# A one-core transformer block: a fixed issue order in place of a list scheduler, with four changes to the work itself

## The chip, the cores and the metric

The kernel runs on one core of a Trainium2 chip. The metric is the device time of one execution in microseconds (us). A run of this program on one core has no second die to compare with; runs are called fast or slow by the spread of the same kernel's times (over 1.5% above its fastest is slow), and only fast runs are compared. The profile's span (first to last instruction) is about 1.7 us shorter than the reported time: 214.4 us against 216.15 us in the profiled run of the kernel before.

Engines in the profile: PE is TensorE's matmuls, PEld its weight loads, DVE is VectorE, ACT is ScalarE, POOL is GpSimd. A name with q (POOLq) is an engine's sequencer.

## The reference

One transformer block in bf16, on x of 2048 rows by 512, modulated by a vector c:

```python
mod = (silu(c) @ w_mod)                       # six rows of 512: sa, ca, ga, sb, cb, gb
h = layernorm(x) * (1 + ca) + sa              # first norm
x = x + ga * A(h)                             # A: 32 heads of 16; each row looks at 8 rows,
                                              #    0, 2, ..., 14 rows back; softmax; @ wo
h = layernorm(x) * (1 + cb) + sb              # second norm
x = x + gb * B(h)                             # B: third norm, then an MLP that mixes ROWS:
                                              #    gelu(h^T @ w1 + b1) @ w2 + b2
                                              #    w1 [2048, 1792], w2 [1792, 2048]
```

The MLP mixes rows, so its first product sums over all 16 tiles of 128 rows, and its gelu cannot start before the last tile has passed the third norm. The 1792 hidden columns are 14 units of 128.

## The kernel before: what the change and the argument touch

The kernel describes its work as operations on engines and lets a list scheduler with hand-tuned ranks (`RANK`, `BIAS`) put them in order and, where it may, choose the engine. Chunks of 2, 4, 4, 4 and 2 tiles pass through norm, QKV, attention and output projection; the sums of MLP1 run in between.

ScalarE computes each 1/sqrt(variance) as Exp(-0.5 Ln(v)), and each softmax's reciprocal as Exp(-Ln(s)). One explicit table load, with nothing to wait for, stands first on ScalarE; the set that it names holds both Ln and Exp:

```python
add("act", 1.3, lambda: nc.scalar.add_instruction(
    mybir.InstLoadActFuncSet(name=..., act_func_set_id=6, ins=[], outs=[])), name="act_table")

def ln_rstd(l, g0, n, name, ...):             # l: which of the three norms
    def fa():
        nc.scalar.activation(lv[:, sl, 0], var, ACT.Ln, bias=epscol[:, 0:1])
        nc.scalar.activation(rs[:, sl, 0], lv[:, sl, 0], ACT.Exp, scale=-0.5)
    add("act", 0.5, fa, ...)
    if vreads is None and "A" not in NE[l][g0:g0 + n]:
        return                                # normalise as (x - mean) * rs
    ...                                       # else nb = -mean * rs, normalise as x * rs + nb

# softmax: (cut)
nc.scalar.activation(ls, ps(s_s)[:, 0:SB], ACT.Ln)
nc.scalar.activation(rb, ls, ACT.Exp, scale=-1.0)
```

`NE` holds a letter for each norm and tile: A for ScalarE, D for VectorE, P for GpSimd. MLP1 is summed in sweeps over tiles; between sweeps a unit's partial sum is parked in SBUF, and taken up again by a matmul with the identity (`inj`) or by an addition on VectorE (`padd`):

```python
BOUNDS=(6, 10)                                # all 14 units are parked after tiles 6 and 10
bounds = [0] + list(BOUNDS) + [NST]
for li, (s_lo, s_hi) in enumerate(zip(bounds[:-1], bounds[1:])):
    ...                                       # load w1's rows, then for each of the 14 units:
    for s in range(s0, s1):
        nc.tensor.matmul(ps(s_), lhsT=w1p[:, s - s_lo, fl * P:(fl + 1) * P], rhs=h3[:, s, :], ...)
...
order = G.schedule()                          # the list scheduler
for o in order:
    o.fn()
```

## Time and profile before

| kernel before | |
|---|---|
| time, median of 3 runs | 216.18 us (216.0 to 216.32) |
| span in the profile | 214.4 us |
| third chunk's row maximum done | 61.68 us |
| last tile normed, last PE stretch begins | 148.99 us |
| work of PE behind it, and tail | 61.5 us and 3.9 us |
| table loads on ScalarE | 2 |

From the page of the kernel before: busy time of each engine, and the chain of work that ended last, by engine.

```profile
PE 201.8 (94%) x1453; PEld 99.9 (47%) x1475; DVE 168.1 (78%) x256; ACT 123.9 (58%) x270; POOL 24.2 (11%) x43
...
PE 73%; DVE 15%; DMA 4%; issue 3%; ACT 1%; POOLq 1%; SPq 1%; DVEq 0%
```

The shares are averages over stages with different limits. The end of the chain of waits of the kernel before shows the last stage (start, duration, engine, tile, instructions):

```profile
143.43 3.28 issue
146.71 2.24 POOLq L1082
148.99 4.26 PE psS L238 x19
...
197.55 12.95 PE psS L238 x73
```

The last norm, on GpSimd, is done at 148.95 us (146.71 + 2.24); PE starts at 148.99 and works without a hole until 210.5. So the span is the time T of the last normed tile, plus the PE work behind it, plus a tail: 149.0 + 61.5 + 3.9. Before T, two engines share the load. The table of windows of the kernel before (window; its length and then the busy us of PE, PEld, DVE, ACT, POOL with their instructions; granted clock; DMA share; GB/s):

```profile
15.00:30.00 15.00, 14.95 (x111) 9.56 (x111) 14.08 (x29) 11.59 (x25) 4.22 (x3) 0.90 1.02 277
30.00:45.00 15.00, 13.99 (x135) 6.55 (x136) 13.12 (x14) 11.44 (x23) 6.12 (x4) 1.00 0.41 98
45.00:60.00 15.00, 14.89 (x139) 6.70 (x138) 14.58 (x9) 10.97 (x22) 0.00 (x0) 1.00 0.99 150
```

PE and VectorE are nearly full; ScalarE has 3 to 4 us free in each 15. The row maximum of each chunk's attention is a good clock hand of this stretch, as it stands between VectorE's products and ScalarE's Exp. In the timeline of VectorE before (start, duration, ...):

```profile
26.39 0.67 DVE L238 TENSOR_REDUCE m<-psL 128x64 bf16<-128x512 f32 x1
47.56 1.22 DVE L238 TENSOR_REDUCE m<-psL 128x128 bf16<-128x1024 f32 x1 [0.36 <-PE psL L238]
60.46 1.22 DVE L238 TENSOR_REDUCE m<-psL 128x128 bf16<-128x1024 f32 x1
```

And the first instructions of ScalarE before; in brackets the idle time ahead of an instruction, and what ended it:

```profile
1.38 1.28 ACT L238 ACT_TABLE_LOAD   x1 [1.38 <-PEq L1071]
4.70 0.29 ACT L238 ACTIVATE lv<-mv,epscol 128x2 f32<-128x2 f32 x1 [2.03 <-POOL stack L238]
5.02 0.20 ACT L238 ACTIVATE rs<-lv 128x2 f32<-128x2 f32 x1
```

`lv` is the Ln of a norm, `rs` its Exp. The table is loaded while ScalarE has nothing else to do, and Exp follows Ln at once.

### The profile page before, as it was taken

How to read it: one execution, taken by the hardware profiler on the slowest of the kernel's cores; microseconds unless marked ns; L12 is line 12 of the kernel's file. 1: busy time of each engine (PE TensorE's matmuls, PEld its weight loads, DVE VectorE, ACT ScalarE, POOL GpSimd, SP SyncE). 2: the span in 40 equal slices, each digit the busy share in tenths (PEclk: the TensorE clock that was granted, in tenths of full speed). 3: DMA queues.
4: the chain of work that ended last, by engine and by line, in shares of the span. 5: the costliest groups of instructions: out<-in, count | busy, mean ns of one | idle time of the engine just before them, and what ended most of it. 6: DMA issues, size and time to landing. Idle time of an engine off the chain costs nothing.

```text
span 214.4 us, 3880 instructions
## 1 busy us (share of the span) xinstructions
PE 201.8 (94%) x1453; PEld 99.9 (47%) x1475; DVE 168.1 (78%) x256; ACT 123.9 (58%) x270; POOL 24.2 (11%) x43
## 2 busy tenths in 40 slices
PE   7599999899999999999999999988999999999992
PEld 7479345335444447443443344333444444444451
DVE  3699999799999999999999789997854445544553
ACT  3548778658789989988857668886852000000000
POOL 6030709100000000000000034034000000000000
PEclk9958999999999999999999999999999999999998
DMA  5999974359999999999999886449879110111011
GB/s 170 355 351 333 206 210 101 90 124 161 148 130 134 134 137 311 134 131 135 223 272 207 220 222 174 127 97 321 203 181 249 49 45 28 54 49 49 24 49 50
DMA packets 54182, 34.24 MB, mean 160 GB/s; under 512 B 18452, under 2 KB 54164, under 8 KB 54164
## 3 DMA queue, kind: packets, MB, share of 16 engines
q1 hardware_dynamic: 54156, 34.00, 74.6%
q8 instruction: 11, 0.18, 0.4%
q14 instruction: 7, 0.06, 0.1%
q10 hardware_dynamic: 8, 0.00, 0.0%
HBM read 22.03 MB, written 2.10 MB: 113 GB/s over the span
## 4 chain that ended last, share of the span: by engine, by line
PE 73%; DVE 15%; DMA 4%; issue 3%; ACT 1%; POOLq 1%; SPq 1%; DVEq 0%
PE psS L238 69%; DVE st L238 4%; DVE h L238 4%; PE psL L238 4%; DVE big L238 4%; DMA xx<-in_A_x_dram 3%; DMA hT<-h 2%; DVE mv L238 1%; POOLq L1082 1%; DVE xx L238 1%; SPq L238 1%; DVE w_qkv L238 0%; ACT lv L238 0%; ACT o_sb L238 0%; ACT k_f L238 0%
## 5 line engine op out<-in xcount | busy, mean ns | idle before, releaser
L238 PE MATMUL psS<-h,wst 128*128 128x512 bf16 x216 | 50.9, 379 | 1.7 <-POOL h L238 1.2
L238 PE MATMUL psS<-hT,w_qkv 128*128 128x512 bf16 (+1 forms) x234 | 47.1, 346 | 1.2 <-DMA hT<-h 0.9
L238 PEld LDWEIGHTS <-wst 128*128 128x128 bf16 x324 | 30.3, 99 | 35.4 <-issue 4.1
L238 PEld LDWEIGHTS <-w_qkv 128*128 128x128 bf16 x282 | 29.8, 114 | 23.7 <-issue 5.8
L238 DVE TENSOR_TENSOR big<-a2sb,vD 128x4096 bf16<-128x4096 bf16 (+1 forms) x20 | 37.0, 1863 | 2.0 <-DMA vD<-v_f 1.5
L238 DVE TENSOR_TENSOR big<-q_sb,k_f 128x4096 bf16<-128x4096 bf16 (+1 forms) x20 | 36.8, 1859 | 0.2 <-ACT k_f L238 0.2
L238 DVE SCALAR_TENSOR_TENSOR h<-psS,bcol,gb_bc 128x512 f32<-128x512 f32 (+1 forms) x17 | 12.2, 719 | 24.6 <-PE psS L238 24.5
L238 ACT ACTIVATE gT<-psS 128x512 bf16<-128x512 f32 x28 | 15.9, 591 | 5.2 <-PE psS L238 5.2
L238 PE MATMUL psS<-gT,big 128*128 128x512 bf16 x83 | 18.2, 379 | 0.1
L238 DVE BATCH_NORM_STATS2 st<-xx 128x6 f32<-128x512 bf16 x21 | 14.2, 675 | 4.2 <-DMA xx<-in_A_x_dram 4.1
L238 PE MATMUL psS<-woq,o_sb 128*128 128x512 bf16 x61 | 16.2, 380 | 0.2
L238 PE MATMUL psS<-gT,wst 128*128 128x512 bf16 (+1 forms) x83 | 15.3, 343 | 0.1
L238 PEld LDWEIGHTS <-big 128*128 128x128 bf16 x116 | 9.2, 98 | 12.3 <-DMA big<-in_w_mod_dram 2.4
L238 ACT ACTIVATE h<-xx,nb,rs 128x512 bf16<-128x512 bf16 x17 | 13.3, 809 | 1.8 <-DVE nb L238 1.7
L238 PEld LDWEIGHTS <-ident 128*128 128x128 bf16 (+1 forms) x146 | 11.1, 110 | 6.8 <-issue 1.7
L238 POOL TENSOR_SCALAR h<-xx,mv,rs 128x512 bf16<-128x512 bf16 x2 | 4.3, 2132 | 87.5 <-DVE xx L238 87.0
L238 ACT ACTIVATE q_sb<-psS,qvb 128x512 bf16<-128x512 f32 (+1 forms) x20 | 11.7, 605 | 4.0 <-PE psS L238 3.9
L238 DVE TENSOR_TENSOR psS<-psS,gT 128x512 f32<-128x512 f32 x14 | 9.2, 695 | 4.6 <-PE psS L238 4.6
L238 ACT ACTIVATE v_f<-psS,qvb 128x512 bf16<-128x512 f32 (+1 forms) x20 | 11.5, 601 | 1.1 <-PE psS L238 0.7
L238 POOL TENSOR_SCALAR h<-xx,rs,nb 128x512 bf16<-128x512 bf16 x7 | 10.3, 1485 | 15.3 <-DMA woq<-in_A_wo_dram 8.6
L238 ACT ACTIVATE k_f<-psS 128x512 bf16<-128x512 f32 x16 | 9.5, 597 | 4.0 <-PE psS L238 3.7
L238 ACT ACTIVATE lv<-mv,epscol 128x1 f32<-128x1 f32 (+2 forms) x25 | 7.3, 292 | 7.9 <-DVE mv L238 5.7
(96 smaller groups left out, 234.9 us busy)
## 6 DMA issues: line engine op xcount, KB each, us to landing
vD<-v_f SPq DMA_DIRECT2D x48, 130.0 KB, 7.4
wst<-in_B_w_dram SPq DMA_DIRECT2D x6, 768.0 KB, 5.6
wst<-in_B_w_dram SPq DMA_DIRECT2D x4, 896.0 KB, 5.8
big<-in_B_w_dram SPq DMA_DIRECT2D x3, 896.0 KB, 6.3
vD<-v_f SPq DMA_DIRECT2D x32, 66.0 KB, 3.6
out_dram<-h SPq DMA_DIRECT2D x15, 128.0 KB, 1.7
xx<-in_A_x_dram SPq DMA_DIRECT2D x3, 512.0 KB, 9.7
gT<-in_w_mod_dram SPq DMA_DIRECT2D x3, 512.0 KB, 9.4
```

Source lines behind the costliest of these rows:

```text
L238: r = fn(*a, **k)
L1082: with _tile.TileContext(nc) as tc:
```

## The change

The list scheduler, its ranks and its timing model are replaced by a table of some 800 names, `ORDER`; the order was evidently found by a search outside the kernel. Four changes of the work come with it:

- Units 0 to 6 of MLP1 are parked after tiles 6 and 10 as before, units 7 to 13 only once, after tile 9: seven `inj` matmuls and seven parkings less.
- The first group of MLP2 is issued in three runs, so that it can start before the last gelus are done; the last output tile is cut into pieces of 256, 128 and 128 columns.
- The four modulation rows, needed on all 128 partitions, were made by 16 broadcast matmuls of 512 columns. Now 64 one-column matmuls give the columns, and a round trip through DRAM spreads them as rows.
- The sums of the second norm are taken on ScalarE for all tiles but 14 and 15 (before: all but 10, 11, 12, 14, 15), and the letters of `NE` change: 14 norms on GpSimd. With them goes a rule: only a group of tiles that is all on VectorE still normalises as (x - mean) * rs; before, a group without ScalarE did, so that GpSimd had norms of both forms.

```diff
     def schedule(self):
-        ops = self.ops
-        ...                                  # list scheduling by ready time and rank (cut)
+        by_name = {o.name: o for o in self.ops}
+        for pos, token in enumerate(ORDER.split()):
+            name, *rest = token.split(":")   # name, and a or d for the engine
+            ...
+            order.append(o)
+ORDER = """
+ident ld_c ld_x_1 ld_x1 ld_x0 consts ld_wmod1 ld_wmod0 ld_wqkv2 cps ld_wqkv0 silu_exp silu_dve ln1s5 ld_wqkv1
+... (cut)
+ld_b1 n1_15 mrowt1 qkv3_10 pv1_1 vd1_31 mrows1:a act_table red2_3 vd1_01 qkv3_20 st_row1 ev3_02:a xt15 qkv3_00
+... (cut)
+"""
-    BOUNDS=(6, 10),
+    MIX=((0, 7, (6, 10)), (7, 14, (9,))),
-    NE=('AADADAPPPAAPPPAP', 'AAAAADDADAPDPAAA', 'DADDDDDDAAAAPDPD'),
-    X1D=(10, 11, 15),
-    LN2D=(10, 11, 12, 14, 15),
+    NE=('DAAADDAAAPAAPAAA', 'APPPAAADAAAPPPPP', 'PPAPAADDAPDADDDD'),
+    X1D=(14, 15),
+    LN2D=(14, 15),
-        if vreads is None and "A" not in NE[l][g0:g0 + n]:
+        if vreads is None and NE[l][g0:g0 + n] == "D" * n:
             return
-                    nc.tensor.matmul(ps(s_), lhsT=sc_rep[:, kt, :], rhs=src[:, kt, :], ...)   # 16 x 512 columns
+                            nc.tensor.matmul(ps(s_)[:, r * KT + dt_:r * KT + dt_ + 1],
+                                             lhsT=w_[:, dt_ * P:(dt_ + 1) * P], rhs=sc[:, kt:kt + 1], ...)
+            dma(scratch rows <- mrows), dma(rows_bc <- scratch, read 128 times)               # shortened
+            runs = [(0, 9), (9, 12), (12, NFT)] if st == 0 else [(0, NFT)]
```

`act_table` stands in `ORDER` after `mrows1:a`. The list scheduler had it first.

## The prediction

> **What bounds the kernel before.** The page gives PE 94%, DVE 78%, ACT 58% of a 214.4 us span. By stage (the table of 6 us windows) there are two limits. From 18 to 149 us DVE is full (5.6 to 6.0 of most windows) and PE nearly so; ACT has slack (46 us busy in the first 66). The chain of waits runs on DVE from 124 to 143, then waits for GpSimd's norm of a last tile until 149.0. After that PE alone counts: 61.5 us of back-to-back 512-column matmuls (219 ns apart), then a 3.9 us tail.
>
> So span = T (last normed tile) + PE work behind it + tail = 149 + 61.5 + 3.9.
>
> **What the change does, costed.**
> - PE: 16 broadcast-row matmuls and 7 injections go (23 x 0.219 = 5.0 us), 64 one-column ones come (2.5 us): -2.5 us, nearly all before T, where PE will have room.
> - DVE before T: three fewer statistics of the second norm (0.8 each), fewer norms; four hT copies and small sums more: about -3 us. ACT takes three sums of squares, GpSimd 14 norms instead of 9 (0.8 us alone, 2.1 when DVE is busy).
> - MLP1 by unit: half the units have a last sweep of 7 tiles, issued as one piece. In PE's order 91 MLP1 and 224 MLP2 matmuls stand behind the last normed tile: 315 x 0.219 = 69 us instead of 61.5, +7.4 us at unchanged T.
> - Split of the first MLP2 group, and 128-column last pieces: about -0.4 us of tail.
> - Table loads: the explicit load of the table with both Ln and Exp stood first on ACT; now it stands behind some 85 ACT instructions, and the built program has 17 table loads instead of 2: until then one before every Ln and every Exp. The Trainium skill ("ScalarE: Activation LUTs", "What ACT_TABLE_LOAD costs") gives 1283 ns plus a drain of 1380; the trace agrees with the first (1.28 us) and shows no such drain. 15 x 1.28 = 19 us more on ACT, all before about 62 us. ACT's slack there was about 20 us, so ACT becomes as full as DVE; each early norm and softmax gets 2.6 us of latency. I estimate the first QKV matmuls 3 us later, and the third chunk's max at 64.5 us (61.6 before). PE may also stay at half clock past 18 us, as its start is emptier.
>
> **Sum.** From the third max DVE needs 77 us (80 before) to the last normed tile, plus 4 to 8 idle (7.6 before): T = 146 to 150. Then 69 + 3.5: span 218 to 222. Without the table loads the same order would give about 212. The order was evidently searched and may pack better than my idle guess; I shade down: 219 us, 80% in 210 to 227. Faster 18%, same 36%, slower 46%.
>
> **What would show it.** ACT_TABLE_LOAD x17; ACT over 90% busy from 15 to 62 us; PE holes early, half clock longer; last normed tile near 147; then an unbroken PE stretch of 69 us; 14 norms on GpSimd; no broadcast-row matmuls.
>
> **What would make it wrong.** Table loads hidden because ACT's queue ran ahead of need (then 212 or less); DVE idle near zero after 60 us; or the last norms, now serial on GpSimd at 2.1 us, or the transfers of v's shifts pushing T beyond 150.

## The result

| | before | after |
|---|---|---|
| time, median | 216.2 us (216.0 to 216.32, 4 runs) | 225.57 us (225.32 to 226.09, 4 runs) |
| ratio of fast runs | 1 | 1.0438 (95%: 1.0415 to 1.046) |
| span in the profile | 214.4 us | 224.1 us |
| third maximum done | 61.68 us | 70.62 us |
| last PE stretch begins (T) | 148.99 us | 152.19 us |
| PE work behind it, and tail | 61.5, 3.9 us | 68.2, 3.7 us |

Ratios here and below are the mean time of one kernel's fast runs over that of the other's fast runs of the same rounds, so not quite the ratio of the medians.

The kernel is 4.4% slower. The same parts of the page, after, and with them the line of one group (count; busy us; mean ns; idle before and what ended it):

```profile
PE 200.9 (90%) x1504; PEld 103.1 (46%) x1528; DVE 166.2 (74%) x265; ACT 135.1 (60%) x281; POOL 19.0 (8%) x45
...
PE 47%; DVE 26%; ACT 15%; issue 7%; DMA 3%; DVEq 0%; ACTq 0%; SPq 0%
...
L131 ACT ACT_TABLE_LOAD x17 | 21.8, 1283 | 6.0 <-DVE mv L131 4.3 <-PEq L989 1.4
```

PE has 0.9 us less to do and the span is 9.7 us longer: this is not a matter of more work on PE. ScalarE's share of the chain went from 1% to 15%. There are 17 table loads. The first instructions of ScalarE after show where:

```profile
1.39 1.28 ACT L131 ACT_TABLE_LOAD   x1 [1.39 <-PEq L989]
...
7.19 1.28 ACT L131 ACT_TABLE_LOAD   x1 [4.33 <-DVE mv L131]
8.48 0.30 ACT L131 ACTIVATE lv<-mv,epscol 128x2 f32<-128x2 f32 x1
8.80 1.28 ACT L131 ACT_TABLE_LOAD   x1
10.09 0.20 ACT L131 ACTIVATE rs<-lv 128x2 f32<-128x2 f32 x1
```

Without the explicit load at the front, the build put a load before every Ln and every Exp until the explicit one comes at 67.16 us: 14 loads in seven pairs. Each holds ScalarE for 1.28 us. The bracket of the second line is worth a look: the load put in before the Ln stands behind the wait for the statistics (`mv`). So it does not run in the 4.33 us in which ScalarE is idle, but after them. (Ahead of the other pairs ScalarE was hardly idle, so only this one shows it.)

The windows after, the maxima after (timeline of VectorE), and a line of the waits over the whole span (engine, what it waited for; us in total, times, longest):

```profile
15.00:30.00 15.00, 12.99 (x82) 9.75 (x85) 10.91 (x36) 12.63 (x23) 2.41 (x5) 1.00 0.56 153
30.00:45.00 15.00, 12.27 (x81) 5.32 (x82) 12.24 (x11) 14.21 (x22) 3.79 (x1) 1.00 0.95 150
45.00:60.00 15.00, 11.99 (x166) 6.27 (x169) 14.15 (x13) 12.94 (x22) 0.00 (x0) 0.94 0.67 116
```

```profile
37.94 0.68 DVE L131 TENSOR_REDUCE m<-psL 128x64 bf16<-128x512 f32 x1
49.88 1.22 DVE L131 TENSOR_REDUCE m<-psL 128x128 bf16<-128x1024 f32 x1
69.40 1.22 DVE L131 TENSOR_REDUCE m<-psL 128x128 bf16<-128x1024 f32 x1
```

```profile
DVE nb L131 <- ACT rs L131: 9.9, 5, 3.6
```

From 15 to 60 us ScalarE is busy 39.8 of 45 us, VectorE 37.3 (41.8 before) and PE 37.3 (43.8 before). No engine is full: they wait for one another. VectorE alone waits 9.9 us for `rs`, nearly all of it for an Exp behind two table loads; in the kernel before this wait is 0.7 us in all. The end of the chain after:

```profile
152.19 7.93 PE psS L131 x36
...
214.13 6.29 PE psS L131 x56
```

From the third maximum to T the kernel after takes 81.6 us (152.19 - 70.62), the kernel before 87.3 (148.99 - 61.68). So 8.9 of the 9.7 us are lost before the third maximum. After it 5.7 us come back before T, and 6.7 us more of PE work stand behind T.

### The profile page after: what moved, and what is told of

Read it like the earlier page. It is cut to its first block, busy times and chain, and to the rows that moved or that the text cites. A ratio compares the mean times of both kernels' runs of the same rounds, so it can differ in the third digit from the quotient of the medians.

```text
span 224.1 us, 3994 instructions
## 1 busy us (share of the span) xinstructions
PE 200.9 (90%) x1504; PEld 103.1 (46%) x1528; DVE 166.2 (74%) x265; ACT 135.1 (60%) x281; POOL 19.0 (8%) x45
## 4 chain that ended last, share of the span: by engine, by line
PE 47%; DVE 26%; ACT 15%; issue 7%; DMA 3%; DVEq 0%; ACTq 0%; SPq 0%
PE psS L131 45%; DVE big L131 11%; DVE st L131 6%; DVE h L131 5%; ACT L131 5%; ACT h L131 3%; DVE mv L131 2%; PE psL L131 2%; DMA xx<-in_A_x_dram 2%; DMA vD<-v_f 1%; ACT q_sb L131 1%; ACT junk L131 1%; DVE m L131 1%; ACT xx L131 1%; ACT lv L131 1%
## 5 line engine op out<-in xcount | busy, mean ns | idle before, releaser
L131 PE MATMUL psS<-hT,w_qkv 128*128 128x512 bf16 (+1 forms) x230 | 47.6, 348 | 3.9 <-ACT k_f L131 2.6
L131 PEld LDWEIGHTS <-wst 128*128 128x128 bf16 x354 | 31.1, 99 | 35.7 <-issue 4.3
L131 DVE SCALAR_TENSOR_TENSOR h<-psS,bcol,rows_bc 128x512 f32<-128x512 f32 (+2 forms) x18 | 12.4, 690 | 23.4 <-PE psS L131 14.7
L131 ACT ACT_TABLE_LOAD x17 | 21.8, 1283 | 6.0 <-DVE mv L131 4.3
L131 PE MATMUL psS<-gT,wst 128*128 128x512 bf16 (+2 forms) x97 | 15.3, 317 | 0.1
L131 ACT ACTIVATE gT<-psS,bcol 128x512 bf16<-128x512 f32 x14 | 8.9, 686 | 10.6 <-DVE psS L131 10.6
L131 ACT ACTIVATE h<-xx,nb,rs 128x512 bf16<-128x512 bf16 x18 | 14.0, 807 | 2.1 <-DVE nb L131 2.0
L131 PEld LDWEIGHTS <-ident 128*128 128x128 bf16 x135 | 11.2, 117 | 4.4 <-issue 1.0
L131 DVE BATCH_NORM_STATS2 st<-xx 128x6 f32<-128x512 bf16 x18 | 12.1, 673 | 1.1 <-DMA xx<-in_A_x_dram 1.1
L131 DVE TENSOR_TENSOR h<-h,xx 128x512 bf16<-128x512 f32 (+2 forms) x18 | 11.4, 633 | 1.6 <-DMA out_dram<-h 1.0
L131 DVE TENSOR_TENSOR h<-h,rows_bc 128x512 bf16<-128x512 bf16 (+2 forms) x20 | 12.0, 601 | 0.3
```

Source lines behind the costliest of these rows:

```text
L131: r = fn(*a, **k)
```

## The experiments

The theory at this point: the late table load is the whole loss. The rival: the other parts (order, parking, rows) cost too, and the loads hide in ScalarE's idle time. All runs gave right results.

| run | based on | table loads more than e1, before the third maximum | ratio to before | third maximum done | T |
|---|---|---|---|---|---|
| after | | 14 in seven pairs, and the explicit one | 1.0438 | 70.62 | 152.19 |
| e1_table_first | after | 0 | 1.0016 | 60.99 | 143.52 |
| e3_seven_loads | e1 | 7, one before each Ln | 1.0019 | 61.60 | 143.16 |
| e9_seven_between | e1 | 7, one between each Ln and Exp | 1.0033 | 62.93 | 144.66 |
| e10_fourteen_away | e1 | 13, outside the pairs | 1.0234 | 66.05 | 147.62 |
| e7_fourteen_same | e1 | 14, two in each pair | 1.0395 | 69.88 | 151.44 |
| e5_table_after_norm2 | after | 4 in two pairs, and the explicit one | 1.0195 | 64.90 | 147.8 |
| e6_table_after_norm4 | after | 8 in four pairs, and the explicit one | 1.0340 | 67.28 | 149.34 |

### Is it the table load?

e1: the token of the load goes to the front.

```diff
-ident ld_c ld_x_1 ...  mrows1:a act_table red2_3 ...
+ident ld_c act_table ld_x_1 ...  mrows1:a red2_3 ...
```

> The changed kernel with one token of its order moved: the explicit table load stands first on ScalarE, so 2 table loads instead of 17. Theory A (the early table loads fill ScalarE and delay everything behind it): the third chunk's max ends near 60 us instead of 70.6, the last normed tile near 140 instead of 152, the PE stretch behind it stays at 68 us, span near 212, ratio to the kernel before 0.965 to 0.995. Rival B (the new order itself loses the time, its packing fails on the chip): ratio stays above 1.02, the third max stays after 67 us.

Measured: 1.0016 (0.9964 to 1.0067), two loads, third maximum at 60.99 us. From its timeline of VectorE (the third maximum) and its chain of waits (the last PE stretch):

```profile
59.77 1.22 DVE L131 TENSOR_REDUCE m<-psL 128x128 bf16<-128x1024 f32 x1
143.52 68.23 PE psS L131 x343
```

The loss is gone, so the rival falls. My own expectation of a gain over the kernel before was missed as well: without the loads the rest of the change is neutral in sum, not a gain. The three maxima of e1 are done at 31.66, 44.43 and 60.99 us; those of the kernel after are 7.0, 6.7 and 9.6 us later. So most of the delay is there by the first maximum, behind the first four pairs, all of them of norms.

e2: the same fault alone, in the kernel before.

```diff
     order = G.schedule()
+    act = next(o for o in order if o.name == "act_table")
+    order.remove(act)
+    order.insert(next(i for i, o in enumerate(order) if o.name == "rcp1") + 1, act)
```

> The kernel before, everything as it was, but its table load moved behind the second softmax's Ln and Exp, so 16 loads appear. Theory A: ScalarE's slack of about 20 us in the first 66 us is eaten, each early norm and softmax gets 2.6 us of latency, third max 6 to 10 us later than 61.6 us, ratio 1.025 to 1.05. Rival B (loads hurt only where the order is packed as tightly as in the changed kernel): ratio below 1.01.

Measured: 1.0590 (1.0554 to 1.0625), more than expected; 16 loads, third maximum at 75.19 us (61.68), T at 162.0 us, and behind it the same 61.5 us of PE. The late load costs the kernel before even more than the kernel after, whatever else is in it. The granted clock fell to a half again in two stretches (28.7 to 32.1 and 42.4 to 45.8 us).

### Why fourteen, and why not seven?

e3: the load at the front, and seven more loads of the same table, one before the Ln of each of the seven early pairs.

```diff
+    def ts_load():
+        nc.scalar.add_instruction(
+            mybir.InstLoadActFuncSet(name=..., act_func_set_id=6, ins=[], outs=[]))
+        ts = ts_load if l == 0 else (lambda: None)
+        add("act", 0.5, lambda: (ts(), fa()), ...)       # first norms: before the Ln
+            if ch < 2: ts_load()                         # softmax of two chunks: before the Ln
```

> The changed kernel with the load first, and seven further explicit loads of the same table, one ahead of each of the first five norms' Ln and the first two softmaxes' Ln (about half of the extra loads, same places). Theory A (the time of the loads on ScalarE counts, whatever they load): about half of the loss between the first experiment and the changed kernel comes back, third max near 65 us, ratio near 1.01. Rival C (changing between two tables is what costs, loading the same one is cheap): loads shorter than 1.28 us, ratio as in the first experiment.

Measured: 1.0019 (0.9992 to 1.0047). Seven loads of 1283 ns each are 9.0 us of ScalarE's time for nothing: cheaper than I expected.

e5 and e6: the changed kernel with the token moved forward only to behind the second norm's or the fourth norm's pair, so that fewer pairs are hit.

```diff
-... rstd1_1 sab ...            mrows1:a act_table ...
+... rstd1_1 act_table sab ...  mrows1:a ...             (e5; in e6 after rstd1_3)
```

> The changed kernel with the explicit table load placed right behind the second norm's Ln and Exp: 7 loads instead of 17, the five extra ones all at the start. If the start is what is expensive (the loads sit on the way to the first QKV matmuls): the third max moves from 61.0 (load first) to about 64, ratio 1.01 to 1.02. If the loads cost only where ScalarE is short of time (15 to 60 us): ratio as with the load first, 1.00.

> The same with the load behind the fourth norm's Ln and Exp: 11 loads, nine extra. If each pair costs about its 2.6 us of latency as long as no pair is hidden: first max near 38 us as in the changed kernel, third max 67 to 69, ratio 1.03 to 1.035. If the later pairs (two softmaxes and a norm after 40 us) are what costs: ratio below 1.02.

Measured: 1.0195 and 1.0340. With the last step to 1.0438 the loss is spread over the pairs: 1.8% for the first two, 1.5% for the next two, 1.0% for the other three. But e5's five loads cost 1.8% more than e1, and e3's seven 0.03%, which is within the noise; so it is not the number of loads alone. The last step has something else in it too: in the kernel after the granted clock is at half from 58.3 to 61.7 us, in e6 it is not. By my estimate 3.4 us at half clock can cost at most 1.7 us of PE's work.

e7: fourteen loads as in the changed kernel, but all of the table that is already there.

```diff
+            if l == 0: ts_load()                        # as e3, and also between Ln and Exp
```

> Explicit load first, and fourteen further explicit loads of that same table, one before each Ln and one before each Exp of the first seven pairs, where the changed kernel has its automatic ones. They differ from those in two ways: they change no table, and the one before an Ln carries no wait, so it can run while ScalarE waits for the statistics. If time on ScalarE is all that counts: as the changed kernel, ratio 1.035 to 1.045, third max 69 to 71. If a load ahead of the wait is free and only the load between Ln and Exp counts: ratio 1.01 to 1.025. If it is the change of table: ratio 1.00.

Measured: 1.0395 (1.0356 to 1.0434), third maximum at 69.88 us. So a change of table is not needed for the loss (the trace does not name the table that a load takes); an instruction of 1.28 us at these places is the cost. Here too the granted clock shows the half-speed stretch at 58.4 to 61.8 us that the kernel after has at 58.3 to 61.7.

Two views make the difference between e3 and e7 plain: ScalarE's timeline of e3 (one load in a pair), and then of e7 (two).

```profile
2.88 1.28 ACT L131 ACT_TABLE_LOAD   x1
7.19 0.30 ACT L131 ACTIVATE lv<-mv,epscol 128x2 f32<-128x2 f32 x1 [3.03 <-DVE mv L131]
7.52 0.20 ACT L131 ACTIVATE rs<-lv 128x2 f32<-128x2 f32 x1
8.76 0.81 ACT L131 ACTIVATE h<-xx,nb,rs 128x512 bf16<-128x512 bf16 x1 [1.04 <-DVE nb L131]
9.59 1.28 ACT L131 ACT_TABLE_LOAD   x1
...
11.65 1.52 ACT L131 ACTIVATE h<-xx,nb,rs 128x512 bf16<-128x512 bf16 x2 [0.23 <-DVE nb L131]
```

```profile
7.17 0.30 ACT L131 ACTIVATE lv<-mv,epscol 128x2 f32<-128x2 f32 x1 [3.01 <-DVE mv L131]
7.49 1.28 ACT L131 ACT_TABLE_LOAD   x1
8.78 0.20 ACT L131 ACTIVATE rs<-lv 128x2 f32<-128x2 f32 x1
9.21 0.81 ACT L131 ACTIVATE h<-xx,nb,rs 128x512 bf16<-128x512 bf16 x1 [0.23 <-DVE nb L131]
10.04 1.28 ACT L131 ACT_TABLE_LOAD   x1
...
13.39 1.52 ACT L131 ACTIVATE h<-xx,nb,rs 128x512 bf16<-128x512 bf16 x2 [0.23 <-DVE nb L131]
```

In e3 the first load, put by hand ahead of the wait, vanishes in ScalarE's idle time, and the first norm has 1.04 us in reserve besides (it waits for `nb`, which VectorE makes from `rs`). In e7 that reserve shrinks to 0.23 us, the smallest bracket seen for this wait, and the second norm comes 1.74 us later. This pair has room for about one load, not for two.

e9 and e10 were made to tell two readings apart: the place of a load inside the pair (latency), or the number of loads (ScalarE's slack in sum).

```diff
             nc.scalar.activation(lv[:, sl, 0], var, ACT.Ln, ...)
+            if l == 0: ts_load()                        # e9: only between Ln and Exp, seven
             nc.scalar.activation(rs[:, sl, 0], lv[:, sl, 0], ACT.Exp, scale=-0.5)

+    for i_ in range(14):                                # e10: as operations of their own,
+        add("act", 1.3, <the same load>, name=f"xl{i_}")  # two behind each pair in ORDER
```

> The changed kernel with its table load at the front (as in e1_table_first, ratio 1.0016), and seven more loads of that same table, each between an Ln and the Exp that follows it in the first seven pairs. e3 put its seven loads before the Ln and cost nothing (1.0019, third maximum done at 61.6 us); e7 had fourteen, before each Ln and each Exp, and cost 3.8% (third maximum 69.9 us). Theory L, latency: a load before an Ln can hide in the engine's wait for the statistics (in e3 it stands before the instruction that carries the wait), a load between Ln and Exp cannot, so these seven are the ones that e7 paid for: ratio 1.025 to 1.04, third maximum 66 to 70 us. Rival S, exhausted slack: only the number of loads counts, seven are absorbed by ScalarE's idle time wherever they stand: ratio 0.997 to 1.01, third maximum 61 to 62.5 us. Between these two: both count.

> The table load at the front and the same number of extra loads as e7 (fourteen), but none of them before an Ln or an Exp of a pair: each stands alone among ScalarE's other work, three and five operations behind each of the first seven pairs. Rival S, exhausted slack of ScalarE: the number alone counts, so 1.03 to 1.045 as e7, third maximum 68 to 71 us. Theory L, latency inside the pairs: 1.00 to 1.015, third maximum 61 to 64 us.

Measured: e9 1.0033 (1.0004 to 1.0062): the strong form of the latency theory falls, as seven loads in the worse place are as good as free. e10 1.0234 (1.0197 to 1.0272), third maximum at 66.05 us: between the two, so neither theory is right alone. The build kept 13 of e10's 14 loads (two had come to stand side by side). From 15 to 60 us ScalarE is busy 43.2 of 45 us in e10, but only 39.1 in e7, which is slower. So about as many loads cost 2.3% by filling ScalarE, and 1.6% more (1.0395 against 1.0234, with one load more) where two stand in one pair. VectorE's wait for `rs` over the whole span (us in total, times, longest) tells the two costs apart; first e7, then e10:

```profile
DVE nb L131 <- ACT rs L131: 9.3, 5, 4.3
DVE nb L131 <- ACT rs L131: 1.5, 2, 1.2
```

In e1 this wait is 0.3 us, in e3 3.9, in e9 2.7. One load in each pair costs VectorE some 3 us of waiting, nearly all of which is caught up; two cost it 9. The 2.3% of e10 lie elsewhere. The clock does not separate the two runs: each has one stretch of 3.4 us at half clock behind its start (29.5 to 32.9 us in e10).

### What is the rest of the change worth?

The four other parts, each alone in the kernel before, with its own scheduler: d1 the rows by DMA, d2 the parking by unit, d3 the letters and the sums on ScalarE, d4 the split of the first and last group of MLP2. And g1: all four together, with the kernel's own scheduler. The edits are those parts of the diff above, but one rule is missing: d3 and g1 keep the old rule for the form of a norm, so that four of their GpSimd norms run as (x - mean) * rs, at 2.07 us and more. So g1 is not quite everything but the table of orders.

> The kernel before with the modulation rows made as columns and spread by DMA, its own scheduler placing everything. 16 matmuls of 512 columns go, 64 of one column come: about 1.5 us of PE less; PE is what is full over the whole span, so ratio 0.99 to 1.00 if the list scheduler packs the rest as well as before; a change of its packing can cost more than that, as it did with the unit-wise sums (1.0575).

> The kernel before with the one part that sets MLP1's sums by unit (units 7 to 13 parked once, after nine tiles), its own scheduler placing everything, table load first. My sum: 7 more matmuls stand behind the last normed tile and the early part of the last sweep is only possible for units 0 to 5, against seven injections and seven evictions saved before it: ratio 1.00 to 1.03. Rival (the part is what makes the changed order good): ratio 0.97 to 0.99.

> The kernel before with the changed kernel's engines for the norms and sums: the second norm's sums on ScalarE for all but two tiles, 14 norms on GpSimd. DVE loses some 3 us of work before the last normed tile, GpSimd gets norms of 2.1 us in a row on the last tiles. If DVE's work bounds the time to the last normed tile: ratio 0.985 to 0.995. If the norms on GpSimd late in the chain of the last tiles decide: 1.00 to 1.02.

> The kernel before with the first MLP2 group split in three and the last tile's group in pieces of 256, 128 and 128 columns, its own scheduler. Tail shorter by 0.2 to 0.5 us; the split of the first group gives nothing where the gelus are done in time. Ratio 0.996 to 1.000.

> The four other parts of the change together (rows by DMA, parking by unit, sums on ScalarE, split first group) in the kernel before with its own list scheduler, that is, everything but the table of orders; the table load is first there. Alone the parts measured 1.0268, 1.0575, 1.0574 and 1.0000. Theory: the parts only pay with an order made for them, and the costs of the single parts are the scheduler's, so together they still cost: 1.03 to 1.12. Rival: the parts complete one another (the freed vector time of one is what the other needs) and the scheduler finds it: 0.99 to 1.01, and then the hand-made table brought nothing but the late table load.

| run | ratio to before | 95% |
|---|---|---|
| d1_rows_alone | 1.0268 | 1.0249 to 1.0288 |
| d2_mix_alone | 1.0575 | 1.0511 to 1.0639 |
| d3_norms_alone | 1.0574 | 1.0555 to 1.0593 |
| d4_tail_alone | 1.0000 | 0.9981 to 1.0019 |
| g1_all_own_scheduler | 1.0829 | 1.0801 to 1.0858 |

None of the parts pays by itself; d1, d2 and d3 cost more than the ranges that were expected. Together under the old ranks they cost 8.3%. The same work in the table of orders, table load first (e1), costs 0.2%. So the table is worth up to 8% to these parts. Part of this may be the missing rule: none of the four slower norms stands in g1's chain of waits, but no run measured them. The likely reason is that the ranks were tuned for the old work; no run tuned them anew. In g1's chain of waits from 78 to 117 us there are DMA waits of 9.0, 7.9 and 6.4 us and a norm on GpSimd; PE is busy only 7.1 us from 105 to 120, all of it at half clock. That norm is a line to remember. The chain of g1, and below it the same instruction in GpSimd's timeline of the kernel after:

```profile
108.70 8.43 POOL h L238
```

```profile
107.24 0.77 POOL L131 TENSOR_SCALAR h<-h,rs,nb 128x512 bf16<-128x512 bf16 x1 [1.53 <-DVE nb L131]
```

One operation, once 0.77 us and once 8.43 us. In g1 VectorE runs three products of 128x4096 bf16 (2.3 us each) and two operations of 128x2048 with `rows_bc` almost back to back during it; in the kernel after it runs statistics. The Trainium skill ("GPSIMD Engine Reference", section "8. Key points") says that GpSimd shares its SBUF interfaces with VectorE and contends with instructions that have two SBUF inputs, which these products have. Durations on GpSimd are rough in a profile, but PE's chain waits for this one, so its end is real. That the contention is the cause is likely and not shown: no run changes it alone.

e8: e1 with the parking of all units after tiles 6 and 10 put back, the order mended by hand.

```diff
-    MIX=((0, 7, (6, 10)), (7, 14, (9,))),
+    MIX=((0, 14, (6, 10)),),
```

> The changed kernel with the table load first and MLP1's sums by unit undone: every unit parked twice, after 6 and 10 tiles, as in the kernel before; the issue order of that stretch written by hand (injection, four matmuls and parking unit after unit; then the early part of the last sweep for units 0 to 5). PE gets 7 injections more (1.5 us), ScalarE 7 evictions more; behind the last normed tile 84 minus up to 24 early matmuls instead of 91. If the unit-wise sums are worth what they save in PE work: slower than with the load first by 1 to 3 us, ratio 1.005 to 1.02. If the 91 matmuls behind the last tile are a real loss: PE stretch behind it near 62 to 64 us instead of 68 and ratio 0.98 to 0.995.

Measured: 1.0192 (1.0159 to 1.0224). Within this order the parking by unit gains; but my mended order was not searched as theirs was, so the difference to e1, some 1.8%, is an upper bound of what the parking itself is worth.

### Attempts at a version that beats both

f1 and f2: e1 with its start reordered, as its first QKV product comes at 16.35 us and that of the kernel before at 12.93 us. f1 brings the first two tiles, their norm and their QKV product ahead of everything else, and adds two bursts of warm-up matmuls; f2 moves the scale column, the first transpose and the first scalings of the weights ahead of VectorE's wait for the second statistics.

```diff
 ... ld_x_4 n1_0                                                        (f2)
+a1col tr0_0 wsc2_2 wsc2_3 rstd1_1 sab hT0_0:d hT0_1:d hT0_2:d hT0_3:d wsc2_0:d wsc2_1:d
 nb1_1 n1_5 ...
```

> A try at a version that beats both: table load first, and the first 15 us reordered: first two tiles of x and the scale's weights loaded first, the scale column taken before the second norm instead of behind it, two more bursts of warm-up matmuls. With the load first the first QKV matmul runs at 16.4 us (12.9 in the kernel before). If the start is what holds the new order at the old time: first QKV near 11 us, third max near 57 to 58, ratio 0.98 to 0.99. If PE or DVE is full from there on anyway and the start is not the limit: ratio 0.995 to 1.005.

> An attempt to beat both kernels. The table load at the front, and in the start of the table of orders the scale column, the first transpose, its copies and the first weight scalings are moved ahead of the wait for the second group's statistics, so that the first QKV product can start about 3 us earlier than in e1_table_first (16.4 us there, 12.9 us in the kernel before). If the start is what holds e1 back: first QKV near 13.5 us, third maximum 58 to 60 us, ratio 0.985 to 0.995. If the first chunks are held by the sum of vector work instead (f1_start gained the start and lost it by the third maximum): first QKV earlier, third maximum 60.5 to 62 us, ratio 0.998 to 1.01.

Measured: f1 1.0135 (1.0079 to 1.0192), f2 1.0117 (1.0087 to 1.0147). Both got the earlier product (10.69 and 14.04 us) and lost it again: their third maxima came at 60.88 and 62.38 us, against 60.99 in e1. The first product is not what the stretch waits for; presumably what VectorE and ScalarE did for it earlier, they did not do for the second chunk. Both were slower than either side of what was expected.

f3 and f4: the kernel before, with the third norm of tile 14 (f3), or of tiles 12 and 14 (f4), on ScalarE in place of GpSimd, where PE stood 0.60 and 0.58 us for them. PE's order is unchanged in f3.

```diff
-    NE=(..., 'DADDDDDDAAAAPDPD'),
+    NE=(..., 'DADDDDDDAAAAPDAD'),       # f3; f4: 'DADDDDDDAAAAADAD'
```

> An attempt to beat both kernels, on the kernel before: the third norm of tile 14 goes from GpSimd to ScalarE, one letter, PE's order unchanged. In the kernel before PE stands 0.60 us before 148.99 us for this norm (2.17 us on GpSimd), and ScalarE is idle for 1.30 us there; the same norm takes 0.80 us on ScalarE. If the span is the time of the last normed tile plus the PE work behind it: PE's hole goes, 0.4 to 0.7 us less, ratio 0.997 (0.995 to 0.999). If the hole is only moved to a later wait: 0.999 to 1.002.

> As f3_last_norm_act, and the third norm of tile 12 (2.07 us on GpSimd, PE stands 0.58 us for it before 143.49 us) on ScalarE too. If each hole of PE there is worth its length: 1.0 to 1.3 us less than before, ratio 0.995 (0.993 to 0.997). ScalarE's later work is pushed back by 0.8 us each, so the rival is a ratio as in f3 or worse: 0.997 to 1.003.

Measured: f3 0.9974 (0.9953 to 0.9996), f4 0.9989 (0.9962 to 1.0015). PE's line at the place in question, in the timeline of the kernel before and of f3:

```profile
148.99 7.28 PE L238 MATMUL psS<-h,wst 128*128 128x512 bf16 x32 [0.60 <-POOL h L238]
```

```profile
148.77 7.50 PE L238 MATMUL psS<-h,wst 128*128 128x512 bf16 x33 [0.39 <-DVE h L238]
```

f3 is 0.26% below the kernel before: the interval just excludes 1, and this is the best of four attempts. The hole became shorter, not nothing: the next wait is there at once, for a norm on VectorE. That is 0.21 us, or 0.1%; the other 0.2 us by which the profiled span is shorter (214.0 against 214.4) are there at the third maximum already (61.46 against 61.68 us), long before the edit acts. So the form "T plus PE's work behind it" is borne out for some 0.1%, and more is not shown. f4 is no gain: its profiled run has 1.2 us less (span 213.2 against 214.4), as expected, but by chance: 1.0 us of it is there at the third maximum (60.72 us), and its two holes of PE came to 0.95 us against 1.18. Its six runs scatter from 215.0 to 217.1 us.

## Why the prediction was right or wrong

**Right.** The direction, though with 46% and a sum only 1.3% above the time before it was no firm call; and the means: 17 table loads, each 1.28 us without a drain behind it, PE with early holes, PE at half clock past 18 us (256-column matmuls of the kernel after are 213 ns apart until 20.7 us and 109 ns after; in the kernel before the step comes at 18 us; the clock column of the windows shows 1.00 here only because the record of the clock begins at 20.8 us), 14 norms on GpSimd. And the later terms of the sum:

| term | predicted | measured |
|---|---|---|
| third maximum done | 64.5 | 70.62 |
| from there to the last normed tile | 77 plus 4 to 8 of idle | 81.57 |
| PE work behind it | 69 | 68.2 |
| tail | 3.5 | 3.7 |

The second row is right in sum only: VectorE was busy 79.6 us of it and idle 2.0, so two errors cancel, which is luck.

**Wrong: the size, by one term.** The step that failed is "I estimate the first QKV matmuls 3 us later, and the third chunk's max at 64.5 us (61.6 before)". It allowed 2.9 us of delay; the chip showed 8.9 (9.6 against e1). The first QKV matmul came 5.0 us later (17.95 against 12.93), but 3.4 of these are the new order's (16.35 in e1) and only 1.6 the loads'; the delay that counts came behind it, and stood at 7.0 us against e1 by the first maximum. The other terms together were about 2 us too high (with 6 us of idle: 83 + 69 + 3.5 against 81.6 + 68.2 + 3.7), so the sum, 220, missed the measured span of 224.1 us by 4.1. Two small slips were added on top: I shaded 220 down to 219, and I put a span beside a time, which is 1.7 us longer.

**Why that term was too small.** The prediction set 19 us of loads against 20 us of ScalarE's slack and, by its 2.9 us, let nearly all of them fit. But slack is not a store that can be drawn on anywhere. e3 and e9 show that about one load for each pair fits (7 loads, 0.2% to 0.3%); e10 shows that 13 don't fit even away from the pairs (2.3%); e7 shows 4.0% for two in each pair, though ScalarE is then only busy 39.1 of 45 us. The prediction named the 2.6 us of latency that each early norm and softmax gets, and then charged for little of it. Nor did ScalarE become "over 90% busy": it was 88% busy from 15 to 60 us, while VectorE waited 9.9 us for its `rs`.

**Also wrong: the estimate of about 212 without the loads.** e1 showed a span of 215.4 us. The longer PE stretch was foreseen (68.2 us in e1); T was not: 143.52 us, where the expectation of e1 says near 140, with 1.0 us of the difference before the third maximum and 2.5 behind it. Against the kernel before, T came 5.5 us earlier, and 6.7 us more of PE work stood behind it (68.2 against 61.5): what was saved before T came back as matmuls behind T. This is why e1 is no faster than the kernel before (1.0016, 0.9964 to 1.0067).

**Left open.** How ScalarE's loss in e10 divides among single waits; and why e2 loses more than the changed kernel with as many loads. In e2 there is more half-clock time and the scheduler's order leans on ScalarE more (34.0 us busy from 15 to 60 us in the kernel before, 31.8 in e1), but no run tells these apart. Nor does any run show what the half-clock stretches cost by themselves: the kernel after, e2, e7 and e10, with 13 loads or more, have them in mid-kernel; e1, e3, e5, e6 and e9 do not.

## What to carry to other kernels

When instructions are put in a fixed order, look for those whose effect is on the build and not on data: here a table load with no reader was free to land anywhere, and its place decided over 15 other loads. Cost a delay by the chain it stands in and not only by an engine's free time in sum: one load for each Ln-Exp pair was free, two were not, although ScalarE had idle time left in both cases; and the sum counts too, as 13 loads outside the pairs cost 2.3%. And an order made for one set of work is worth little for another: the same four parts cost 8.3% under the old ranks (with GpSimd's old form of norms) and 0.2% under an order made for them.

## What the Trainium skill lacked or had wrong

- "ScalarE: Activation LUTs", section "What ACT_TABLE_LOAD costs": the 1283 ns agree (1283 ns mean in every run). The drain of about 1380 ns that it adds to a switch was not seen: in the kernel after the load ends at 10.08 us and the Exp starts at 10.09. The page speaks of a switch to a different set, and which set these loads name the trace does not show; loading the set that is already active took the same 1283 ns (e3, e7).
- The same page, section "Table sets: the hidden batching unit", says that ln(x) then exp(x) needs one load, as one set has both. That held only with the explicit load in front (2 loads); left to itself the build put a load before each Ln and each Exp, 14 in seven pairs. "ScalarE activation tables: per-element evaluation and per-set limits", section "Table sets in the compiler and the runtime", says that loads are placed by the greedy longest run; these pairs, whose functions share a set, don't fit that.
- No page that I read says where a load put in by the build stands to a wait: in the first pair of the kernel after it stands behind the wait, so that it cannot hide in it (4.33 us idle, then 1.28 us of load).
- "GPSIMD Engine Reference", section "8. Key points", names the contention with VectorE but no size, and I found none for this pair of instructions in another page: 0.77 us became 8.43 us for one 128x512 norm, if contention it was. The form counts as well, which no page that I read says: x * rs + nb took 0.76 us at best, (x - mean) * rs never under 2.07 us.
- "TensorE: Matmul & The Clock Gate", table under "Why this matters for your kernels", warns of idle gaps over about 3 us. By this row alone the kernel after would have kept its clock, but it fell to half for 3.4 us from 58.3 us on; the longest gap between the starts of two matmuls from 50 us to there was 2.11 us (up to 54.15 us), and in the 7 us from 51 to 58 PE was busy 5.2.
